# Cosformer attention into a gated feed-forward: the opening block's sums, copies and gate products in another order

## The chip, the cores and the metric

The kernel runs on one core of one Trainium2 chip. The metric is the time of one execution on the device in microseconds (us), lower is better. The engines named here are PE (TensorE: matrix products, transposes, each with a weight load PEld), DVE (VectorE), ACT (ScalarE), POOL (GpSimd) and SP (SyncE, which here only issues transfers).

## The reference

Eight batches of eight heads, 576 positions, head width 64. The attention has no softmax: with r = max(x, 0), a row of q or k becomes 128 features, r times a cosine and r times a sine of its position. Then a feed-forward layer with a norm in front works on the 4608 x 512 result.

```python
q_p, k_p = phi(q, cos_w, sin_w), phi(k, cos_w, sin_w)      # 128 features
kv  = einsum('bhsf,bhsd->bhfd', k_p, v)
z   = sum(k_p, axis=2)
num = einsum('bhsf,bhfd->bhsd', q_p, kv)
den = einsum('bhsf,bhf->bhs', q_p, z)[..., None] + 1e-06
x   = (num / den) as 4608 x 512
xn  = x / sqrt(mean(x*x) + 1e-6) * rms_g
out = (silu(xn @ w_gate) * (xn @ w_val)) @ w_out           # 512 -> 1536 -> 512
```

## The kernel before

The order of every engine's work is written out by hand (`manual_schedule`): each engine takes its instructions in the order in which the program names them, and waits only for what the data and the buffers ask. The work goes in blocks of 512 rows: one for each batch, and one with the eight tails of 64 rows. A block in its steady form is 12 gate products and 12 value products (`gval_mm`, 4 matmuls of 512 columns each, through the PSUM banks `psG[0/1]` and `psV[0/1]`), a silu on ACT and a product on DVE for each (`gval_h`), and then 48 matmuls against `w_out`. The attention of the next batch is put between these by hand (`at`, `run`).

Block 0 has no such cover. Its attention has to be done before its first products, and the program text of the opening does it in this order.

- `k_phi` makes the features of k in nine parts `c` (cosine half on DVE, sine half on ACT, the last two sine halves on DVE). `z0_pe(c)` adds each up over the rows with a matmul against ones into two banks, `psC[1]` and `psV[1]`. `g_spread`, after part 4, spreads the norm weight over the partitions (12 small matmuls into `psC[0]`).
- `q_phi` and `q_tr_pe` make and turn the first two of the four row groups j of q. `q_tr_evac` on DVE copies them out.
- `z0_copy` (ACT, twice, L389) takes the sums out as a row; `kv0_pe` makes k'v for the four head pairs hp (72 matmuls, L404) in the two banks of `psA`; `z0_turn` (8 small matmuls, L394) puts the sums beside it; `kvz_evac` (ACT, L277) copies both banks.
- For each j: `nd0_pe` (numerator and denominator into `psA`, L426 and L432), `nd_post` = `nd_rec` + `nd_div` on DVE (L455, L467; x into `xt`), `x_sq` (square sum on ACT, the power -0.5 on POOL, L483 and L488), `x_norm` on DVE (L495), `x_tr_pe` (turn, PE, L514), `x_tr_evac` (copy into `xnT`, L279 or L277).
- `filler` is a matmul on zeros whose result nobody reads.

The products of block 0 start before all its rows are ready. They go in units, `units[i]` = row groups j0 to j1 and columns of w_gate and w_val: units 0 to 3 are rows 0 and 1 against column groups 0-4 and 4-8, units 4 to 7 are rows 2 and 3 together against two column groups each. `unit_mm(i, wg)` is the gate product of a unit into `psG[i % 2]`, `unit_mm(i, wv)` the value product into `psV[i % 2]`, `unit_silu` and `unit_h` are its ACT and DVE steps (L622, L626), and all the matmuls are on L611.

The weights come from HBM in three parts for each matrix, column groups 0-4, 4-8 and 8-12, all issued by POOL (L174) in one order with the loads of q, k and v: wg 0-4, wv 0-4, wg 4-8, wv 4-8, k of batch 1, wg 8-12, wv 8-12, q and v of batch 1, then w_out in three parts.

After unit 3 the order before was: units 4, 5, 6, 7, each gate product, value product, silu, product, then `gval_step` for column groups 8 to 11.

Of the kernel before, what the change touches and what calls it, by code (L numbers as in the profile page):

```python
# [9 lines left out]
FP32 = mybir.dt.float32  # L10
BF16 = mybir.dt.bfloat16
# [6 lines left out]
def kernel(  # L18
# [11 lines left out]
    nc = tc.nc  # L30
    B, H, S, D = q.shape
    DM = H * D
    DFF = moe_w_gate.shape[1]
    P = 128
    TB = 512
    HP = H // 2
    NC = S // 64
# [3 lines left out]
    NDT = DM // P  # L41
    NNT = DFF // P
    E = D + 1
    F = 2 * D
    assert B == 8 and H == 8 and S == 576 and D == 64 and DFF == 1536

    V, A, G = nc.vector, nc.scalar, nc.gpsimd
# [2 lines left out]
    one = ctx.enter_context(tc.tile_pool(name="one", bufs=1))  # L50
    ring = ctx.enter_context(tc.tile_pool(name="ring", bufs=5))
    two = ctx.enter_context(tc.tile_pool(name="two", bufs=2))
    three = ctx.enter_context(tc.tile_pool(name="three", bufs=3))
    four = ctx.enter_context(tc.tile_pool(name="four", bufs=4))
    six = ctx.enter_context(tc.tile_pool(name="six", bufs=6))
    ps = ctx.enter_context(tc.tile_pool(name="ps", bufs=1, space=bass.MemoryType.PSUM))

    psA = ps.tile([P, 2, 512], FP32, name="psA")
# [132 lines left out]
    def g_parts():  # L191
        rest = g4
        for i in range(3):
            V.tensor_copy(out=g3[:, i, :], in_=rest[:, :])
            if i < 2:
                V.tensor_tensor(
                    out=gres[:, i, :], in0=rest[:, :], in1=g3[:, i, :], op=ALU.subtract
                )
                rest = gres[:, i, :]
# [19 lines left out]
    load_kv("k", 1, eng=G)  # L219
    load_w(wg, moe_w_gate, 8, NNT)  # L220

    def g_spread(bank):
        for t in range(NDT):
            for i in range(3):
                nc.tensor.matmul(
                    bank[:, t * P : (t + 1) * P], lhsT=sel[:, t, :], rhs=g3[:, i, :],
                    start=(i == 0), stop=(i == 2),
                )

    ang = math.pi / 2.0 / float(S)  # L230
    fidx = one.tile([P, NTAB], FP32, name="fidx")
# [43 lines left out]
    def copy(eng, o, i):  # L275
        if eng is A:
            A.copy(out=o, in_=i)  # L277
        else:
            eng.tensor_copy(out=o, in_=i)  # L279
# [10 lines left out]
    def k_phi(eng, b, c, part, hps=(0, HP)):  # L290
        o = slice(0, D) if part == 0 else slice(D, F)
        f = cos_of if part == 0 else sin_of
        if wide(b):
            rows = rows_of(c)
            src = raw_kv("k", b)[0:rows, :, c * D : (c + 1) * D]
            phi(eng, kp5[0:rows, c, :, o], src, f(14 + c)[0:rows, :])
            return
        src = raw_kv("k", b)[:, hps[0] : hps[1], c * D : (c + 1) * D]
        phi(eng, kp[:, c, hps[0] : hps[1], o], src, f(c))
# [39 lines left out]
    def q_tr_evac(eng, b, j, bank):  # L339
        dst = bank.bitcast(BF16).rearrange("p (h s) -> p h s", h=H)  # L340
        copy(eng, qpT[:, :, j * P : (j + 1) * P], dst)
# [12 lines left out]
    kvzs = {}  # L354
# [21 lines left out]

    zbank = [psC[1], psV[1]]
    zrow = one.tile([1, 2, HP * F], BF16, name="zrow")

    def z0_pe(c):  # L380
        for g in range(2):
# [3 lines left out]
                start=(c == 0), stop=(c == NC - 1),  # L385
            )

    def z0_copy(g):
        A.copy(out=zrow[:, g, :], in_=zbank[g][0:1, :])  # L389

    def z0_turn():
        for hp in range(HP):
            for g in range(2):
                nc.tensor.matmul(  # L394
                    heads[:, g, hp, D:E], lhsT=zrow[:, g, hp * F : (hp + 1) * F],
                    rhs=ones[0:1, 0:1], start=False, stop=(hp == HP - 1),
                    skip_group_check=True,
                )

    def kv0_pe(hp):  # L400
        for c in range(NC):
            for g in range(2):
                lo, hi = 64 * g, 64 * g + 64
                nc.tensor.matmul(  # L404
                    heads[:, g, hp, 0:D], lhsT=kp[lo:hi, c, hp, :],
                    rhs=vv0[lo:hi, hp, c * D : (c + 1) * D],
                    start=(hp == 0 and c == 0), stop=False, skip_group_check=True,
                )

    def kvz_evac(eng, b):  # L410
        kvzs[b] = six.tile([P, 2, HP * E], BF16, name="kvzs", tag="kvzs")
        copy(eng, kvzs[b][:, :, :], psA[:, :, 0 : HP * E])
# [39 lines left out]
    def nd_rec(b, j):  # L452
        rec = four.tile([P, 2, HP], FP32, name="rec", tag="rec")
        if b == 0 and j < 4:
            V.reciprocal(out=rec[:, :, :], in_=heads[:, :, :, D])  # L455
        else:
            V.tensor_scalar(
                out=rec[:, :, :], in0=heads[:, :, :, D], scalar1=1e-6, scalar2=None, op0=ALU.add
            )
            V.reciprocal(out=rec[:, :, :], in_=rec[:, :, :])  # L460
        rec_of[(b, j)] = rec

    def nd_div(b, j):
        xt = xts[count["x"] % NXT]
        count["x"] += 1
        rec = rec_of[(b, j)]
        V.tensor_tensor(  # L467
            out=xt[:, 0:DM].rearrange("p (hp g d) -> p g hp d", g=2, d=D),
            in0=heads[:, :, :, 0:D],
            in1=rec[:, :, :].unsqueeze(3).to_broadcast([P, 2, HP, D]),  # L470
            op=ALU.mult,
        )
        x_of[(b, j)] = xt

    def nd_post(b, j):
        nd_rec(b, j)
        nd_div(b, j)
# [13 lines left out]
    def x_norm(b, j, cols=(0, DM)):  # L491
        if cols[0] == 0:
            xn_of[(b, j)] = four.tile([P, DM], BF16, name="xn", tag="xn")
        c = slice(*cols)
        V.scalar_tensor_tensor(  # L495
            out=xn_of[(b, j)][:, c], in0=x_of[(b, j)][:, c], scalar=rs_of[(b, j)][:, :],
            in1=gb[:, c], op0=ALU.mult, op1=ALU.mult,
        )
# [11 lines left out]
    def x_tr_pe(b, j, bank, ts=(0, NDT)):  # L510
        xn = xn_of[(b, j)]
        dst = bank.bitcast(BF16).rearrange("p (t s) -> p t s", s=P)
        for t in range(*ts):
            nc.tensor.transpose(dst[:, t, :], xn[:, t * P : (t + 1) * P], ident[:, :])  # L514

    def x_tr_evac(eng, b, j, bank, ts=(0, NDT)):
        dst = bank.bitcast(BF16).rearrange("p (t s) -> p t s", s=P)
        copy(eng, x_dst(b, j)[:, ts[0] : ts[1], :], dst[:, ts[0] : ts[1], :])
# [20 lines left out]

    def gval_h(blk, n):  # L540
        g, v = banks_of(blk, n)
        sg = three.tile([P, TB], FP32, name="sg", tag="sg")
        A.activation(out=sg[:, :], in_=g[:, 0:TB], func=AF.Silu)  # L543
        V.tensor_tensor(out=hT[:, n, :], in0=v[:, 0:TB], in1=sg[:, :], op=ALU.mult)  # L544

# [21 lines left out]
    def filler(n, bank):  # L567
        for _ in range(n):
            nc.tensor.matmul(
                bank[:, :], lhsT=warm[:, 0:P], rhs=warm[:, :], start=True, stop=True  # L570
            )


    g_parts()
    filler(10, psC[1])
    for c in range(NC):
        k_phi(V, 0, c, 0)
        k_phi(A if c < 7 else V, 0, c, 1)
        z0_pe(c)
        if c == 4:  # L580
            g_spread(psC[0])
    qbank = [psG[0], psG[1], psV[0], psV[1]]
    for j in range(2):
        q_phi(V, 0, j, 0)
        q_phi(A, 0, j, 1)
        q_tr_pe(0, j, qbank[j])
    for j in range(2):
        q_tr_evac(V, 0, j, qbank[j])
    z0_copy(0)
    z0_copy(1)  # L590
    A.copy(out=gb[:, :], in_=psC[0][:, :])
    for hp in range(HP):
        kv0_pe(hp)
    z0_turn()
    kvz_evac(A, 0)

# [19 lines left out]
            )  # L618

    def unit_silu(i):  # L620
        sg_of[i] = three.tile([P, TB], FP32, name="sg", tag="sg")
        A.activation(out=sg_of[i][:, :], in_=psG[i % 2][:, 0:TB], func=AF.Silu)  # L622

    def unit_h(i):
        j0, j1, n0, n1 = units[i]
        V.tensor_tensor(  # L626
            out=hT[:, n0:n1, j0 * P : j1 * P],
            in0=psV[i % 2][:, 0:TB].rearrange("p (n s) -> p n s", n=n1 - n0),
            in1=sg_of[i][:, :].rearrange("p (n s) -> p n s", n=n1 - n0), op=ALU.mult,
        )  # L630

    HALF = DM // 2
    lo, hi = (0, NDT // 2), (NDT // 2, NDT)
    filler(3, psC[1])
    nd0_pe(0)
    q_phi(V, 0, 2, 0)
    q_phi(G, 0, 3, 0)
    q_phi(A, 0, 2, 1)
    q_phi(A, 0, 3, 1)
    filler(2, psC[1])  # L640
    nd_post(0, 0)
    q_tr_pe(0, 2, qbank[2])
    filler(1, psC[1])
# [1 line left out]
    load_w(wv, moe_w_val, 8, NNT)  # L645
    nd0_pe(1)
    q_tr_evac(V, 0, 2, qbank[2])
    filler(1, psC[1])
    q_tr_pe(0, 3, qbank[3])
    nd_post(0, 1)  # L650
    filler(2, psC[1])
    nd0_pe(2)
    x_sq(0, 1)
    load_q(1, eng=G)
# [4 lines left out]
    filler(1, psG[1])  # L659
    x_tr_pe(0, 0, psC[1], hi)  # L660
    x_tr_evac(A, 0, 0, psC[0], lo)
    q_tr_evac(A, 0, 3, qbank[3])
    nd_rec(0, 2)
    x_tr_evac(V, 0, 0, psC[1], hi)
    x_norm(0, 1)
    nd_div(0, 2)
    filler(2, psG[1])
    unit_mm(0, wg, by_rows=True)
    x_tr_pe(0, 1, psC[0])
# [5 lines left out]
    nd0_pe(3)  # L675
    nd_post(0, 3)
    x_norm(0, 2)
    unit_h(0)
    unit_mm(1, wg)
    unit_mm(1, wv)  # L680
    x_sq(0, 3)
# [1 line left out]
    load_wo(8, 12)  # L683
    unit_silu(1)
    x_norm(0, 3)
    x_tr_pe(0, 2, psC[1])
    x_tr_evac(V, 0, 2, psC[1])
    unit_h(1)
    unit_mm(2, wg)
    unit_mm(2, wv)  # L690
    x_tr_pe(0, 3, psC[0])
    x_tr_evac(V, 0, 3, psC[0])

    slots = {}

# [133 lines left out]
        out_store(A, blk, j, bank)  # L829
        run(blk, n, "post")  # L830

    for i in range(2, len(units)):
        if i > 2:
            unit_mm(i, wg)
            unit_mm(i, wv)
        unit_silu(i)
        unit_h(i)
        run(0, i, "post")
    for n in range(8, NNT):
# [37 lines left out]
```

## Time and profile before

| | us |
|---|---|
| median of 3 runs (lowest to highest) | 325.4 (324.87 to 326.1) |
| the profiled execution, its own time | 325.76 |
| its span, first to last instruction | 324.0 |
| PE busy in the span | 317.4 |
| DVE, ACT, POOL busy | 184.3, 165.2, 40.7 |

A timeline line gives start, duration, engine, source line, operation, output <- inputs and, in brackets, the idle time of the engine ahead of it and what ended it. Where one line stands for several instructions (x16), matmuls are pipelined: a group's duration is longer than the distance to the next group, and the distance is what the group costs PE.

### The profile page before, as it was taken

To read this page: it belongs to the slowest core of one execution; us is meant where nothing else is said; L and a number is where in the kernel's file an instruction comes from. 1 tells how busy PE (TensorE), PEld (TensorE's weight loads), DVE (VectorE), ACT (ScalarE), POOL (GpSimd) and SP (SyncE) were. 2 spreads that over 40 slices of the span, in tenths; PEclk is the share of its full clock that TensorE was granted. 3 is DMA by queue.
4 is the path that set the end of the run, shared out by engine and by line. 5 is a ranking of instruction groups with operands and counts; after the bars stand their busy time and mean duration, and the time that the engine had idled before them with its cause. 6 is when DMAs were issued, how large, how long until landed. Compare 5 with 4: busy or idle time off the path is not lost.

```text
span 324.0 us, 6128 instructions
## 1 busy us (share of the span) xinstructions
PE 317.4 (98%) x2348; PEld 163.7 (51%) x2348; DVE 184.3 (57%) x379; ACT 165.2 (51%) x319; POOL 40.7 (13%) x78
## 2 busy tenths in 40 slices
PE   7989999999999999999999999999999999999996
PEld 3679665544454445444454445444544444444444
DVE  7784858757727774576557745782577034204410
ACT  5664856754574547445754575446643343223321
POOL 9771212001000110011001000110011000000000
PEclk9999999999999999999999999999999999999999
DMA  7999995999579966998699958995822300041002
GB/s 228 231 266 273 281 327 212 228 204 259 125 178 216 231 193 159 200 229 210 171 205 214 211 149 182 223 200 144 134 49 41 123 32 0 2 98 32 2 32 97
DMA packets 77627, 53.37 MB, mean 165 GB/s; under 512 B 50410, under 2 KB 71326, under 8 KB 77598
## 3 DMA queue, kind: packets, MB, share of 16 engines
q1 hardware_dynamic: 70374, 39.81, 57.0%
q0 software_dynamic: 7216, 13.17, 16.5%
q8 instruction: 18, 0.29, 0.4%
q14 instruction: 11, 0.09, 0.1%
q10 hardware_dynamic: 8, 0.00, 0.0%
HBM read 37.83 MB, written 9.44 MB: 146 GB/s over the span
## 4 chain that ended last, share of the span: by engine, by line
PE 92%; DMA 5%; POOL 2%; issue 0%; DVE 0%; POOLq 0%
PE psC L547 27%; PE psG L524 27%; PE psV L524 27%; DMA wv<-in_moe_w_val_dram 5%; PE psA L417 2%; PE psG L547 2%; PE psA L361 2%; PE psV L611 2%; PE psG L611 1%; PE psA L368 1%; POOL raw L124 1%; PE psA L442 0%; POOL wg L174 0%; POOL vv L204 0%; PE psC L337 0%; PE psV L514 0%
## 5 line engine op out<-in xcount | busy, mean ns | idle before, releaser
L544 DVE TENSOR_TENSOR hT<-psV,sg 128x512 bf16<-128x512 f32 x100 | 68.9, 689 | 102.2 <-PE psV L524 65.9
L543 ACT ACTIVATE sg<-psG 128x512 f32<-128x512 f32 x100 | 59.2, 592 | 63.2 <-PE psG L524 63.2
L524 PE MATMUL psV<-xnT,wv 128*128 128x512 bf16 x352 | 90.3, 379 | 0.0
L524 PE MATMUL psG<-xnT,wg 128*128 128x512 bf16 x352 | 90.3, 379 | 0.0
L547 PE MATMUL psC<-wo,hT 128*128 128x512 bf16 (+1 forms) x408 | 89.1, 376 | 0.0
L547 PEld LDWEIGHTS <-hT 128*128 128x128 bf16 x456 | 42.8, 98 | 47.1
L524 PEld LDWEIGHTS <-wv 128*128 128x128 bf16 x400 | 39.1, 98 | 47.2
L524 PEld LDWEIGHTS <-wg 128*128 128x128 bf16 x400 | 37.1, 98 | 39.7
L488 POOL TENSOR_TENSOR rs<-ms,mhalf 128x1 f32<-128x1 f32 x36 | 19.8, 551 | 195.9 <-ACT scr L483 195.9
L277 ACT COPY osb<-psC 128x512 f32<-128x512 f32 x32 | 18.8, 586 | 50.0 <-PE psC L547 50.0
L483 ACT ACTIVATE scr<-xt 128x513 bf16<-128x513 f32 x36 | 22.8, 634 | 24.5 <-DVE xt L467 24.5
L495 DVE SCALAR_TENSOR_TENSOR xn<-xt,rs,gb 128x512 bf16<-128x512 f32 (+1 forms) x37 | 26.9, 730 | 9.7 <-POOL rs L488 9.7
L283 ACT ACTIVATE kp<-raw,tab 128x256 bf16<-128x256 f32 (+2 forms) x50 | 28.4, 609 | 2.5 <-DMA raw<-in_k_dram 2.5
L467 DVE TENSOR_TENSOR xt<-psA,rec 128x512 f32<-128x512 f32 x36 | 24.9, 691 | 1.2
L283 ACT ACTIVATE qp<-raw,tab 128x512 bf16<-128x512 f32 x32 | 22.6, 713 | 1.1 <-DMA raw<-in_q_dram 1.0
L285 DVE TENSOR_SCALAR kp<-raw,tab 128x256 bf16<-128x256 f32 (+2 forms) x54 | 20.3, 421 | 0.7 <-DMA raw<-in_k_dram 0.7
L285 DVE TENSOR_SCALAR qp<-raw,tab 128x512 bf16<-128x512 f32 x31 | 15.3, 498 | 1.6 <-DMA raw<-in_q_dram 1.6
L417 PEld LDWEIGHTS <-qpT 128*128 128x128 bf16 x224 | 10.5, 97 | 6.6 <-issue 0.5
L524 PE MATMUL psG<-xnT_tail,wg 128*128 128x512 bf16 x48 | 12.3, 379 | 0.0
L524 PE MATMUL psV<-xnT_tail,wv 128*128 128x512 bf16 x48 | 12.3, 379 | 0.0
L417 PE MATMUL psA<-kvzs,qpT 128*128 128x65 bf16 x224 | 11.4, 193 | 0.0
L279 DVE CAST vv<-raw 116x1280 bf16<-116x1280 f32 (+1 forms) x13 | 10.5, 805 | 0.0
(95 smaller groups left out, 181.0 us busy)
## 6 DMA issues: line engine op xcount, KB each, us to landing
out_dram<-osb SPq DMA_DIRECT2D x31, 256.0 KB, 2.4
raw<-in_k_dram SPq DMA_DIRECT2D x5, 1120.0 KB, 8.1
raw<-in_v_dram SPq DMA_DIRECT2D x5, 1120.0 KB, 7.7
raw<-in_q_dram SPq DMA_DIRECT2D x5, 1024.0 KB, 9.0
raw<-in_k_dram POOLq DMA_DIRECT2D x2, 1152.0 KB, 19.5
raw<-in_v_dram POOLq DMA_DIRECT2D x2, 1152.0 KB, 15.9
raw<-in_q_dram POOLq DMA_DIRECT2D x2, 1024.0 KB, 16.0
wg<-in_moe_w_gate_dram POOLq DMA_DIRECT2D x3, 512.0 KB, 14.7
```

What stands on the lines that cost most here:

```text
L277: A.copy(out=o, in_=i)
L283: A.activation(out=out_ap, in_=in_ap, func=AF.Relu, scale=scale)
L285: eng.tensor_scalar(out=out_ap, in0=in_ap, scalar1=scale, scalar2=0.0, op0=ALU.mult, op1=ALU.max)
L417: nc.tensor.matmul(heads[:, g, hp, :], lhsT=qpT[:, h, j * P : (j + 1) * P], rhs=kvzs[b][:, g, hp * E : (hp + 1) * E], start=True, stop=True,)
L467: V.tensor_tensor(out=xt[:, 0:DM].rearrange("p (hp g d) -> p g hp d", g=2, d=D), in0=heads[:, :, :, 0:D], in1=rec[:, :, :].unsqueeze(3).to ...
L483: A.activation(out=scr[:, :], in_=xt[:, 0 : DM + 1], func=AF.Square, scale=1.0 / math.sqrt(DM), accum_out=ms[:, :],)
L488: G.tensor_tensor(out=rs[:, :], in0=ms[:, :], in1=mhalf[:, :], op=ALU.pow)
L495: V.scalar_tensor_tensor(out=xn_of[(b, j)][:, c], in0=x_of[(b, j)][:, c], scalar=rs_of[(b, j)][:, :], in1=gb[:, c], op0=ALU.mult, op1=ALU. ...
L524: nc.tensor.matmul(bank[:, cols[0] : cols[1]], lhsT=w[:, t, n * P : (n + 1) * P], rhs=x[:, t, cols[0] : cols[1]], start=(t == 0), stop=(t ...
L543: A.activation(out=sg[:, :], in_=g[:, 0:TB], func=AF.Silu)
L544: V.tensor_tensor(out=hT[:, n, :], in0=v[:, 0:TB], in1=sg[:, :], op=ALU.mult)
L547: nc.tensor.matmul(bank[:, 0 : cols[1] - cols[0]], lhsT=hT[:, n, j * P : (j + 1) * P], rhs=wo[:, n, cols[0] : cols[1]], start=(n == 0), st ...
```

## The change

- `z0_copy` takes an engine: the sums in `psV[1]` are copied by DVE, those in `psC[1]` by ACT. `z0_turn` comes between the second and third head pair of `kv0_pe`.
- k'v and the sums of batch 0 are made in `psG[0]` and `psG[1]` and no longer in `psA`; each bank is copied by an engine of its own (`kvz0_evac`: ACT 0, DVE 1). The first two turns of q use the two banks of `psA` in their place.
- The sine half of k's part 7 moves from DVE to ACT.
- `g_spread` is cut into four parts of three matmuls, behind `z0_pe` of parts 0 to 3.
- The nine fillers between k'v and the turn of x's row group 0 are spread anew over their five places: 3, 2, 1, 1, 2 before; 2, 3, 1, 2, 1 after.
- `nd_rec(0, 2)` moves on DVE from ahead of the second half's `x_tr_evac` of row group 0 to behind `x_norm(0, 1)`.
- From unit 1 on: the gate products of units 2, 3 and 4 come ahead of the value products of units 2 and 3, the gate product of unit 5 ahead of the value product of unit 4. On DVE `unit_h(0)` goes behind the `x_tr_evac` of row group 2, `unit_h(1)` behind that of row group 3. The silu's ring has four buffers where it had three.

```diff
-    def g_spread(bank):
-        for t in range(NDT):
-            for i in range(3):
...
+    def g_spread(bank, t):
+        for i in range(3):
...
+    heads0 = [b[:, 0 : HP * E].rearrange("p (hp e) -> p hp e", e=E) for b in psG]
-    def z0_copy(g):
-        A.copy(out=zrow[:, g, :], in_=zbank[g][0:1, :])
+    def z0_copy(eng, g):
+        copy(eng, zrow[:, g, :], zbank[g][0:1, :])
...
+    def kvz0_evac(eng, g):
...
+        copy(eng, kvzs[0][:, g, :], psG[g][:, 0 : HP * E])
...
+    qbank = [psA[:, 0, :], psA[:, 1, :], psV[0], psV[1]]
-        k_phi(A if c < 7 else V, 0, c, 1)
+        k_phi(A if c < 8 else V, 0, c, 1)
         z0_pe(c)
-        if c == 4:
-            g_spread(psC[0])
-    qbank = [psG[0], psG[1], psV[0], psV[1]]
+        if c < NDT:
+            g_spread(psC[0], c)
...
-    for j in range(2):
-        q_tr_evac(V, 0, j, qbank[j])
-    z0_copy(0)
-    z0_copy(1)
+    z0_copy(V, 1)
+    z0_copy(A, 0)
+    q_tr_evac(V, 0, 0, qbank[0])
+    q_tr_evac(V, 0, 1, qbank[1])
     A.copy(out=gb[:, :], in_=psC[0][:, :])
-    for hp in range(HP):
-        kv0_pe(hp)
+    kv0_pe(0)
+    kv0_pe(1)
     z0_turn()
-    kvz_evac(A, 0)
+    kv0_pe(2)
+    kv0_pe(3)
+    kvz0_evac(A, 0)
+    kvz0_evac(V, 1)
...
+    x_tr_evac(V, 0, 0, psC[1], hi)
     q_tr_evac(A, 0, 3, qbank[3])
-    nd_rec(0, 2)
-    x_tr_evac(V, 0, 0, psC[1], hi)
     x_norm(0, 1)
-    nd_div(0, 2)
+    nd_post(0, 2)
...
     x_norm(0, 2)
-    unit_h(0)
     unit_mm(1, wg)
     unit_mm(1, wv)
...
     x_norm(0, 3)
+    unit_mm(2, wg)
     x_tr_pe(0, 2, psC[1])
     x_tr_evac(V, 0, 2, psC[1])
-    unit_h(1)
-    unit_mm(2, wg)
-    unit_mm(2, wv)
+    unit_silu(2)
+    unit_h(0)
+    unit_mm(3, wg)
     x_tr_pe(0, 3, psC[0])
     x_tr_evac(V, 0, 3, psC[0])
+    unit_silu(3)
+    unit_h(1)
+    unit_mm(4, wg)
+    for i in range(2, 4):
+        unit_mm(i, wv)
+        unit_h(i)
+    unit_silu(4)
+    unit_mm(5, wg)
+    unit_mm(4, wv)
+    unit_silu(5)
+    unit_h(4)
...
-    for i in range(2, len(units)):
-        if i > 2:
+    for i in range(5, len(units)):
+        if i > 5:
             unit_mm(i, wg)
-            unit_mm(i, wv)
-        unit_silu(i)
+            unit_silu(i)
+        unit_mm(i, wv)
         unit_h(i)
```

More of the change, by code (lines that the diff above doesn't have):

```diff
@@ L52 @@
     two = ctx.enter_context(tc.tile_pool(name="two", bufs=2))
-    three = ctx.enter_context(tc.tile_pool(name="three", bufs=3))
     four = ctx.enter_context(tc.tile_pool(name="four", bufs=4))
@@ L220 @@
     load_w(wg, moe_w_gate, 8, NNT)
-    def g_spread(bank):
-        for t in range(NDT):
-            for i in range(3):
[L225 to L228, printed above, removed]
+    def g_spread(bank, t):
+        for i in range(3):
+            nc.tensor.matmul(
+                bank[:, t * P : (t + 1) * P], lhsT=sel[:, t, :], rhs=g3[:, i, :],
+                start=(i == 0), stop=(i == 2),
+            )
     ang = math.pi / 2.0 / float(S)
@@ L394, in z0_turn @@
                 nc.tensor.matmul(
-                    heads[:, g, hp, D:E], lhsT=zrow[:, g, hp * F : (hp + 1) * F],
-                    rhs=ones[0:1, 0:1], start=False, stop=(hp == HP - 1),
-                    skip_group_check=True,
+                    heads0[g][:, hp, D:E], lhsT=zrow[:, g, hp * F : (hp + 1) * F],
+                    rhs=ones[0:1, 0:1], start=False, stop=False, skip_group_check=True,
                 )
@@ L404, in kv0_pe @@
                 nc.tensor.matmul(
-                    heads[:, g, hp, 0:D], lhsT=kp[lo:hi, c, hp, :],
+                    heads0[g][:, hp, 0:D], lhsT=kp[lo:hi, c, hp, :],
                     rhs=vv0[lo:hi, hp, c * D : (c + 1) * D],
-                    start=(hp == 0 and c == 0), stop=False, skip_group_check=True,
-                )
+                    start=(hp == 0 and c == 0), stop=(hp == HP - 1 and c == NC - 1),
+                    skip_group_check=True,
+                )
+    def kvz0_evac(eng, g):
+        if 0 not in kvzs:
+            kvzs[0] = six.tile([P, 2, HP * E], BF16, name="kvzs", tag="kvzs")
+        copy(eng, kvzs[0][:, g, :], psG[g][:, 0 : HP * E])
     def kvz_evac(eng, b):
@@ L541, in gval_h @@
         g, v = banks_of(blk, n)
-        sg = three.tile([P, TB], FP32, name="sg", tag="sg")
+        sg = four.tile([P, TB], FP32, name="sg", tag="sg")
         A.activation(out=sg[:, :], in_=g[:, 0:TB], func=AF.Silu)
@@ L620, in unit_silu @@
     def unit_silu(i):
-        sg_of[i] = three.tile([P, TB], FP32, name="sg", tag="sg")
+        sg_of[i] = four.tile([P, TB], FP32, name="sg", tag="sg")
         A.activation(out=sg_of[i][:, :], in_=psG[i % 2][:, 0:TB], func=AF.Silu)
@@ L633 @@
     lo, hi = (0, NDT // 2), (NDT // 2, NDT)
-    filler(3, psC[1])
+    filler(2, psC[1])
     nd0_pe(0)
@@ L639 @@
     q_phi(A, 0, 3, 1)
-    filler(2, psC[1])
+    filler(3, psC[1])
     nd_post(0, 0)
@@ L647 @@
     q_tr_evac(V, 0, 2, qbank[2])
-    filler(1, psC[1])
+    filler(2, psC[1])
     q_tr_pe(0, 3, qbank[3])
     nd_post(0, 1)
-    filler(2, psC[1])
+    filler(1, psC[1])
     nd0_pe(2)
```

## The prediction

> **What bounds the kernel now.** I read the page's chain first, then the chain piece by piece, then the timelines of PE, DVE and ACT from 8 to 35 us. The page gives the chain to PE, with one transfer in it.
>
> ```profile
> PE 92%; DMA 5%; POOL 2%; issue 0%; DVE 0%; POOLq 0%
> ```
>
> Piece by piece, the opening's place in the chain (start, length, what):
>
> ```profile
> 6.87 0.74 POOL wg L174
> 7.61 16.79 DMA wv<-in_moe_w_val_dram
> 24.40 0.05 issue
> 24.45 1.07 PE psV L611 x16
> ```
>
> So the second part of w_val, issued at 7.61, lands at 24.40, and from there to the end the chain is PE's own work. Nothing ahead of 24.40 that is not that transfer sets the time now. PE's timeline shows what it costs; the windows answer (PE, PEld, DVE, ACT, POOL busy, granted clock, DMA share) shows that PE is full afterwards.
>
> ```profile
> 20.29 1.05 PE L611 MATMUL psG<-xnT,wg 128*128 128x128 bf16 x16
> 21.18 1.06 PE L611 MATMUL psV<-xnT,wv 128*128 128x128 bf16 x16
> 22.12 0.40 PE L514 MATMUL psC<-ident,xn 128*128 128x128 bf16 x4
> 22.35 1.06 PE L611 MATMUL psG<-xnT,wg 128*128 128x128 bf16 x16
> 24.45 1.07 PE L611 MATMUL psV<-xnT,wv 128*128 128x128 bf16 x16 [1.04 <-DMA wv<-in_moe_w_val_dram]
> 25.35 0.39 PE L514 MATMUL psC<-ident,xn 128*128 128x128 bf16 x4
> 25.57 1.06 PE L611 MATMUL psG<-xnT,wg 128*128 128x128 bf16 x16
> ...
> 30.85 1.04 PE L611 MATMUL psG<-xnT,wg 128*128 128x256 bf16 x8
> ```
>
> ```profile
> 25.50:31.00 5.50, 5.50 (x71) 5.13 (x69) 2.41 (x4) 2.02 (x4) 0.76 (x1) 1.00 1.20 249
> ```
>
> A unit of 16 matmuls takes PE 0.89 us (20.29 to 21.18), one of 8 wide ones 0.87, four turns 0.22. Unit 2's gates start at 22.35 and are issued by 23.24; its values start at 24.45. The hole is 1.21 us, the only PE wait over 0.33 us behind 5.6 us. After it unit 6 starts at 30.85 and PE has no other wait on an engine or transfer.
>
> **Part 1, ahead of the units (to 17.87): worth nothing.** The second half of q arrives late, and DVE and ACT both stand still for it:
>
> ```profile
> 13.41 0.48 DVE L285 TENSOR_SCALAR qp<-raw,tab 128x512 bf16<-128x512 f32 x1 [1.64 <-DMA raw<-in_q_dram]
> 13.94 0.21 DVE L455 RECIPROCAL rec<-psA 128x8 f32<-128x8 f32 x1
> ```
>
> ```profile
> 12.76 0.59 ACT L277 CAST kvzs<-psA 128x520 bf16<-128x520 f32 x1 [0.97 <-PE psA L394]
> ```
>
> - The copy of k'v in two halves: DVE copies 128x256 f32 from PSUM in 0.42 and 128x128 in 0.29 (osb rows), so 260 columns take 0.43; ACT's 128x128 and 128x512 take 0.27 and 0.59, so 260 take 0.38. Both end by 13.19, where the one copy ended at 13.35: 0.16 earlier for `nd0_pe(0)`. But DVE's next step, `nd_rec(0, 0)`, stands behind the `q_phi` that waits for q until 13.41 and runs to 13.9. It starts at 13.94 all the same. Gain 0; 0.16 if q came earlier in another execution.
> - `z0_copy` on DVE: like DVE's 128x512 copy from PSUM, 0.69, from 9.95 (after `q_phi`) to 10.64. The two q copies behind it (0.65 apart) end at 11.95 where they ended at 11.76. Their reader, `nd0_pe(0)`, is at 13.2: cover 1.2. `z0_turn` comes after 36 of 72 k'v matmuls, at 10.97 + 0.7 = 11.7, 1.0 after its rows. Cost 0. Without the cover it would be 0.19.
> - k's part 7 on ACT (0.49, in ACT's idle 1.02 ahead of 9.03) takes 0.35 from DVE, but both then wait for q's first half at 9.03. `g_spread` in parts is the same 12 matmuls, 0.77 in all (7.59 to 8.36), and PE waits ahead of 9.80 for ACT's q features anyway. Gain and cost 0.
> - The fillers: nine in both. One less ahead of `nd0_pe(2)` saves up to 0.2 there, but the second half of `x_norm(0, 0)`, which DVE ends at 17.26, sets the turns at 17.33 and so unit 0. 0 again.
> - `nd_rec(0, 2)`, 0.21, ran in a DVE idle of 0.25 (waiting for turns at 17.64); now it is behind `x_norm(0, 1)` and pushes `nd_div(0, 2)` to 19.45 and the copy of row group 1 to 19.46 to 19.88. Readers: unit 1's gates at 20.29 (cover 0.36), `nd0_pe(3)` at 19.99 (cover 0.5), `x_sq(0, 2)`, 0.2 later, and behind it on POOL the first issue for w_out, 20.9. Its landing takes 20.0 to 21.1, so by 42.0; it is read from 43.95. The two later w_out issues follow `x_sq(0, 3)` and w_val's landing, which stay; the second can land at 43.96 (22.86 + 21.1), is read from 44.8 and after the gain below from 44.3. POOL's other queue and SP's are as before.
>
> **Part 2, the units.** From unit 1's value products at 21.18, with the distances above:
>
> - unit 2 gates 22.07 to 22.96. Part 4-8 of w_gate must be there: issued at 6.80, w_gate's median landing 14.7, so 21.5; in the trace it is only sure that it was there at 22.35 (0.28 is the bound on a loss here).
> - turns of row group 2 to 23.19, unit 3 gates to 24.08, turns of row group 3 to 24.30.
> - unit 4's gates need row group 3 copied. DVE's queue now:
>
> ```profile
> 22.93 0.75 DVE L495 SCALAR_TENSOR_TENSOR xn<-xt,rs,gb 128x512 bf16<-128x512 f32 x1 [0.27 <-POOL rs L488]
> 23.60 0.42 DVE L279 COPY xnT<-psC 128x512 bf16<-128x512 bf16 x1
> 23.93 0.68 DVE L626 TENSOR_TENSOR hT<-psV,sg 128x512 bf16<-128x512 f32 x1
> 25.77 0.42 DVE L279 COPY xnT<-psC 128x512 bf16<-128x512 bf16 x1 [1.16 <-PE psC L514]
> ```
>
> The first three keep their times (the product is now unit 0's). The last was 0.2 behind the end of its turns (25.57), so it is possible from 24.50, free at 24.54, done at 24.96. PE goes on 0.05 later (as 13.35 to 13.40): 25.01. **A new hole of 0.71** (24.30 to 25.01) takes the place of the old. Of it 0.67 is the copy's own latency; only 0.04 is the product ahead in DVE's queue. This copy was hidden behind unit 3 before; that cover is gone.
>
> - From 25.01: unit 4 gates 0.87, unit 2 values 0.89 (start 25.88, 1.48 after w_val's landing), unit 3 values 0.89, unit 5 gates 0.87, unit 4 values 0.87, unit 5 values 0.87: 5.26. Unit 6 starts at 30.27, not 30.85. No bank holds it: unit 2's values need `unit_h(0)` (24.6), unit 4's need `unit_h(2)` (27.7, used at 28.5).
>
> Sum: 0.58 earlier on PE, which then runs full, so the span goes from 324.0 to 323.4 and the profiled 325.76 to 325.2. That execution is 0.36 above the median. If its surplus was a late w_val, the median of before had a hole of 0.85, while the new hole does not depend on w_val until it is 1.5 later; then the new time is 325.2 as well. If the surplus was elsewhere, it is 324.8. I take 325.0.
>
> **A rule weighed.** The row: granted clock 1.00 in every window, the one with the 1.21 hole too; the first fillers follow each other at 0.43 until 4.04 and at about 0.22 afterwards, so PE's start is half as fast. The Trainium skill, "TensorE: Matmul & The Clock Gate", "A second HAM failure mode: psum-queue depth-cycling", speaks against the change: frequent small idle stretches between groups that cycle through PSUM banks can let the clock fall. The page's window is about 3.4 us, so one fall would cost about 1.7 by its figures, an estimate. I keep the row's answer: a longer hole left the clock up.
>
> **The rivals.**
> - *The wait comes back elsewhere* (0.17): w_gate's part lands nearer 22.35, or w_out's second part holds PE at 44.3, or the copy of row group 3 is late by 0.3 to 0.5. For it: DMA share 1.0 to 1.2 all through, the covers are 0.3 to 0.6. Then 325.3 to 325.8, 325.5.
> - *The hole closes altogether* (0.08): the copy hides and the whole 1.21 is gained: 324.2 against the median, 324.55 by the profiled run. Against: the copy's latency alone is 0.67.
> - *Slower: PE's clock falls in the opening* (0.15). Place: PE now ends the sums at about 9.1 and idles 0.7 to 9.8, where it idled 0.33; a second idle of 0.71 is at 24.3. Price from the first fillers: 1.17 to 4.04, 2.87 us, at half speed is 1.4 lost. One such stretch behind 17.87 makes 325.0 + 1.4 = 326.4, two 327.8. It decides once turns follow each other at twice the 0.056 of now (0.89 for 16). Against: the 0.7 idle from 4.85 to 5.55 and the hole of 1.21 brought none.
>
> **How the numbers follow.** The forecast, 324.6 to 325.4, has 0.60. The range goes from the closed hole at 324.2 to one slow stretch at 326.5; what is left out is part of the slow case and scatter. Half a per cent, 1.63 us, is about what a measurement of this kernel can tell from no change: faster means under 323.8, which even the closed hole misses, 0.07 for an earlier chain that I do not see; slower means over 327.0, most of the slow case, 0.12; within, 0.81.
>
> **What would show it.** Right: no PE wait on w_val; a PE gap of about 0.7 ahead of unit 4's gates, released by DVE's copy on L277 of the new file; unit 0 still at about 17.9; unit 6 near 30.3; no idle after. Wrong: unit 0 starts over 0.3 away from 17.87, unit 4's gates after 25.6, PE idle beyond 31, or distances of 0.43 between 512-column matmuls after 5 us.

## The result, and the profile after

The changed kernel takes 324.9 us (median of 22 runs, 324.42 to 325.51), the kernel before 325.42 (22 runs, 324.79 to 326.3): a ratio of 0.9982, 95% interval 0.9974 to 0.999. That is 0.52 us or 0.16% faster by the medians: within the half per cent that the prediction called no change, and yet the interval leaves 1 out. The profiled execution took 324.66 with a span of 322.9.

The page's chain, by engine, after. The w_val transfer was 5% of it. Now 2% is a transfer (q's), and 2% is DVE:

```profile
PE 93%; DMA 2%; DVE 2%; issue 1%; POOL 0%; ACT 0%; ACTq 0%; POOLq 0%
```

The chain piece by piece (start, length, what) names the new links. Where w_val's transfer stood, there is now the way of x's row group 3: its norm, its turn's copy, and between them in DVE's queue the product of unit 0.

```profile
21.81 0.57 POOL rs L492
22.41 0.75 DVE xn L499
23.16 0.33 DVE xnT L277
23.49 0.60 DVE hT L633
24.09 0.34 DVE xnT L277
24.48 1.05 PE psG L618 x8
```

PE's timeline from unit 1's value product on:

```profile
20.66 1.06 PE L618 MATMUL psV<-xnT,wv 128*128 128x128 bf16 x16
21.55 1.06 PE L618 MATMUL psG<-xnT,wg 128*128 128x128 bf16 x16
22.45 0.39 PE L518 MATMUL psC<-ident,xn 128*128 128x128 bf16 x4
22.67 1.06 PE L618 MATMUL psG<-xnT,wg 128*128 128x128 bf16 x16
23.56 0.39 PE L518 MATMUL psC<-ident,xn 128*128 128x128 bf16 x4
24.48 1.05 PE L618 MATMUL psG<-xnT,wg 128*128 128x256 bf16 x8 [0.53 <-DVE xnT L277]
25.36 1.95 PE L618 MATMUL psV<-xnT,wv 128*128 128x128 bf16 x32
27.15 1.04 PE L618 MATMUL psG<-xnT,wg 128*128 128x256 bf16 x8
28.02 1.91 PE L618 MATMUL psV<-xnT,wv 128*128 128x256 bf16 x16
29.77 1.04 PE L618 MATMUL psG<-xnT,wg 128*128 128x256 bf16 x8
```

The last line is unit 6. The turns of row group 3 are issued by 23.56 + 0.22 = 23.78, unit 4's gates start at 24.48: a hole of 0.70, released by DVE's copy. No wait on w_val is left; unit 2's values follow unit 4's gates without one (25.36). Behind it PE has no wait on another engine or a transfer, as before.

One thing in this profile misleads. Unit 0 starts at 17.46, 0.41 earlier than in the profile of before, and it is tempting to credit the opening's edits with it. Timelines of ACT, before and after (the first q features):

```profile
9.03 1.33 ACT L283 ACTIVATE qp<-raw,tab 128x512 bf16<-128x512 f32 x2 [1.02 <-DMA raw<-in_q_dram]
```

```profile
8.62 1.33 ACT L281 ACTIVATE qp<-raw,tab 128x512 bf16<-128x512 f32 x2 [0.38 <-DMA raw<-in_q_dram]
```

q's first half itself landed 0.41 earlier. Whether the change did that is the first question for the experiments.

### The profile page after: what moved, and what is told of

Its sections match the earlier page's. It is cut to its first block, busy times and chain, and to the rows that moved or that the text cites. A ratio compares the mean times of both kernels' runs of the same rounds, so it can differ in the third digit from the quotient of the medians.

```text
span 322.9 us, 6078 instructions
## 1 busy us (share of the span) xinstructions
PE 315.6 (98%) x2312; PEld 163.5 (51%) x2348; DVE 185.5 (57%) x380; ACT 164.9 (51%) x319; POOL 40.6 (13%) x78
## 4 chain that ended last, share of the span: by engine, by line
PE 93%; DMA 2%; DVE 2%; issue 1%; POOL 0%; ACT 0%; ACTq 0%; POOLq 0%
PE psV L528 27%; PE psC L551 27%; PE psG L528 26%; PE psA L421 2%; DMA raw<-in_q_dram 2%; PE psG L551 2%; PE psV L618 2%; PE psA L359 2%; PE psG L618 1%; PE psA L366 1%; DVE xn L499 1%; PE psV L335 0%; PE psA L446 0%; DVE xt L471 0%; PE psG L402 0%
## 5 line engine op out<-in xcount | busy, mean ns | idle before, releaser
L528 PE MATMUL psG<-xnT,wg 128*128 128x512 bf16 x338 | 88.6, 379 | 0.6 <-issue 0.2
```

Source lines behind the costliest of these rows:

```text
L528: nc.tensor.matmul(bank[:, cols[0] : cols[1]], lhsT=w[:, t, n * P : (n + 1) * P], rhs=x[:, t, cols[0] : cols[1]], start=(t == 0), stop=(t ...
```

## The experiments

Theory A: the order of the units makes the whole gain, by putting a hole of 0.70 where one of 1.2 to 1.3 was; the opening's edits are worth nothing; when q lands is scatter. Rival B: the opening's edits moved q's landing. Rival C: the removed hole is mostly smaller than the profile shows. Rivals D and E are in the expectations.

The profiles of all kernels, in us. "q" is the start of the first q features on ACT, units 0 and 6 are the starts of their gate products, the hole is PE's gap ahead of unit 2's values (in before's order, and with unit 2's values first) or ahead of unit 4's gates; it is counted from the time by which PE has issued what stands in front (the idle in a line's brackets starts up to 0.17 later, at the modelled end of the last matmul). The last two rows are the last experiment.

| kernel | q | unit 0 | unit 6 | q to unit 0 | unit 0 to 6 | hole | span less q |
|---|---|---|---|---|---|---|---|
| before | 9.03 | 17.87 | 30.85 | 8.84 | 12.98 | 1.21 | 315.0 |
| before, again | 8.37 | 17.32 | 30.30 | 8.95 | 12.98 | 1.31 | 315.0 |
| opening's edits alone | 9.16 | 17.97 | 30.98 | 8.81 | 13.01 | 1.34 | 314.9 |
| changed kernel | 8.62 | 17.46 | 29.77 | 8.84 | 12.31 | 0.70 | 314.3 |
| units' order alone | 8.90 | 17.75 | 30.06 | 8.85 | 12.31 | 0.70 | 314.3 |
| before, no wait on w_val | 8.76 | 17.61 | 29.27 | 8.85 | 11.66 | none | 313.6 |
| changed, no wait for row group 3 | 8.79 | 17.61 | 29.22 | 8.82 | 11.61 | none | 313.5 |
| unit 2's values first | 8.73 | 17.56 | 29.36 | 8.83 | 11.80 | 0.18 | 313.8 |
| changed kernel, again | 8.94 | 17.76 | 30.07 | 8.82 | 12.31 | 0.70 | 314.3 |
| unit 2's values first, again | 8.27 | 17.24 | 28.99 | 8.97 | 11.75 | 0.08 | 313.8 |
| before, no wait for q's second half | 8.78 | 17.62 | 30.33 | 8.84 | 12.71 | 0.90 | 314.7 |
| opening's edits, no wait for q's second half | 9.03 | 17.63 | 30.56 | 8.60 | 12.93 | 0.89 | 314.7 |

**The kernel before once more**, unchanged.

> The kernel before once more, for its profile alone. Theory A (the new order of the units made the gain; the 0.41 us by which unit 0 started earlier in the changed kernel's profile is scatter of q's transfers): the two halves of q may start the q features anywhere from 8.6 to 9.1 and 13.0 to 13.4 us, unit 0 follows at 17.4 to 17.9, and w_val's second part lands 23.5 to 24.5. Rival B (the opening's edits made q land earlier): q's features start at 9.03 and 13.41 again, within 0.05, and unit 0 at 17.87.

Measured: 325.21. q's features start at 8.37 and 12.86 and unit 0 at 17.32, with no edit at all. PE's line at w_val:

```profile
23.89 1.07 PE L611 MATMUL psV<-xnT,wv 128*128 128x128 bf16 x16 [1.15 <-DMA wv<-in_moe_w_val_dram]
```

q came 0.66 earlier than in the first profile, earlier than in the changed kernel's, and w_val came earlier with it (the products that waited for it start at 23.89, not 24.45). Rival B's ground is gone: the 0.41 is within what two profiles of one kernel differ by.

**The units' order alone.** The kernel before with the last part of the change's diff (from `x_norm(0, 2)` on) and the silu's ring of four:

```diff
+    unit_mm(2, wg)
     x_tr_pe(0, 2, psC[1])
     x_tr_evac(V, 0, 2, psC[1])
-    unit_h(1)
-    unit_mm(2, wg)
-    unit_mm(2, wv)
+    unit_silu(2)
+    unit_h(0)
+    unit_mm(3, wg)
     x_tr_pe(0, 3, psC[0])
...
```

> The kernel before with the new order of the units alone (gate products of 2, 3, 4 ahead of value products 2, 3; the silu's ring of four), its opening as it was. A: nearly the whole gain, 0.4 to 0.6 us under before, 324.8 to 325.0; no PE wait on w_val, a hole of about 0.7 ahead of unit 4's gates. B: only what is not the opening's 0.41, so 0.1 to 0.2 under before.

Measured: 324.93 against 325.34 of before on the same chip, ratio 0.9989 (0.998 to 0.9998). Its wait, from PE's waits (who, for what: us in total, times, longest), and its place:

```profile
PE psG L610 <- DVE xnT L278: 0.5, 1, 0.5
```

```profile
24.77 1.05 PE L610 MATMUL psG<-xnT,wg 128*128 128x256 bf16 x8 [0.54 <-DVE xnT L278]
```

The same 12.31 from unit 0 to unit 6, the same hole. This is the change's gain, all of it that a profile can resolve.

**The opening's edits alone.** The changed kernel with the order of the units of before (the same part of the diff, taken back; the silu's ring of four stays).

> The changed kernel with the order of the units of before: the opening's edits alone. A: within 0.15 us of before; PE waits for w_val as before, 0.7 to 1.2. B: 0.3 to 0.5 us faster, if w_val's landing moves with q's; if it does not, the same as before with a longer wait on w_val.

Measured: 325.33 against 325.34, ratio 1.0 (0.9991 to 1.0009). A holds; PE waits for w_val longer than ever:

```profile
24.57 1.07 PE L618 MATMUL psV<-xnT,wv 128*128 128x128 bf16 x16 [1.18 <-DMA wv<-in_moe_w_val_dram]
```

**The kernel before without the wait.**

```diff
     def unit_mm(i, w, by_rows=False):
+        sh = 4 if i == 2 and w is wv else 0
...
-                lhsT=w[:, t, n * P : (n + 1) * P],
+                lhsT=w[:, t, (n - sh) * P : (n - sh + 1) * P],
```

> The kernel before, in which unit 2's value product reads w_val's columns 0-4, which landed long before, in place of 4-8 (so a part of h is another product). It takes the wait on w_val away and nothing else. A: faster by the mean hole, 0.85 to 1.2 us, 324.2 to 324.6. Rival C (the hole is mostly smaller than in the one profile, since w_val lands earlier in other executions): 0.3 to 0.7 faster.

Measured: 324.3 against 325.34, ratio 0.9971 (0.996 to 0.9983). Unit 2's values follow its gates without a wait:

```profile
21.98 1.06 PE L612 MATMUL psG<-xnT,wg 128*128 128x128 bf16 x16
22.87 1.06 PE L612 MATMUL psV<-xnT,wv 128*128 128x128 bf16 x16
```

That is 1.04 faster by the medians (0.55 to 1.30 by the interval) and 1.32 by the distance from unit 0 to 6. Rival C, in which the hole is mostly smaller than in the one profile, falls in its strong form, a gain of 0.3 to 0.7: three profiles of the old order have holes of 1.21, 1.31 and 1.34, although q moved by 0.8 between them. Its direction is not excluded, since in the two profiles of the last experiment the hole is 0.90 and 0.89, and 1.04 lies between.

**The changed kernel without its new hole.**

```diff
     def unit_mm(i, w, by_rows=False):
+        sh = 2 if i == 4 and w is wg else 0
...
-                rhs=xnT[0][:, t, j0 * P : j1 * P],
+                rhs=xnT[0][:, t, (j0 - sh) * P : (j1 - sh) * P],
```

> The changed kernel, in which unit 4's gate product reads row groups 0 and 1 in place of 2 and 3 (so a part of h is another product): it does not wait for the copy of row group 3. A: the new hole of 0.7 us goes and nothing takes its place, since w_val lands 6.55 us after unit 0's start and unit 2's values then start 7.2 after it: unit 6 starts 11.65 us after unit 0, 324.2 to 324.4, 1.0 to 1.2 under before. Rival D (behind the hole another wait is next, w_val or a bank): 324.6 to 324.9.

Measured: 324.12 against 325.38 of before on the same chip, ratio 0.9963 (0.995 to 0.9977). Unit 4's gates follow the turns at once and unit 2's values follow them without a wait:

```profile
23.71 0.39 PE L518 MATMUL psC<-ident,xn 128*128 128x128 bf16 x4
23.94 1.04 PE L619 MATMUL psG<-xnT,wg 128*128 128x256 bf16 x8
24.81 1.95 PE L619 MATMUL psV<-xnT,wv 128*128 128x128 bf16 x32
```

12.31 becomes 11.61: the hole's 0.70, all of it, with no other wait behind it. Rival D falls for this place. So the change took 1.3 of waiting out and put 0.7 back in; nothing else moved by more than 0.1.

**Unit 2's values ahead of unit 4's gates.** The version that the two runs before point to: what PE has ready while DVE copies row group 3 is unit 2's value product, if its bank is free.

```diff
     x_norm(0, 2)
+    unit_h(0)
...
     unit_silu(2)
-    unit_h(0)
+    unit_h(1)
     unit_mm(3, wg)
...
     unit_silu(3)
-    unit_h(1)
-    unit_mm(4, wg)
-    for i in range(2, 4):
-        unit_mm(i, wv)
-        unit_h(i)
+    unit_mm(2, wv)
+    unit_h(2)
+    unit_mm(4, wg)
+    unit_mm(3, wv)
+    unit_h(3)
     unit_silu(4)
```

> A version of the change: unit 2's value product between the turn of row group 3 and unit 4's gate product, unit_h(0) and unit_h(1) back ahead of the copies of row groups 2 and 3 on DVE. A: the copy of row group 3 is hidden behind the value product, w_val's landing (6.55 us after unit 0's start) leaves a hole of 0.2 to 0.3 ahead of unit 2's values: unit 6 about 11.9 after unit 0, 324.3 to 324.5, faster than both kernels. Rival D: the wait on w_val is as long as the hole that it replaces (0.6 or more) and the time is the changed kernel's, 324.8 to 325.0.

Measured: 324.39 against 325.38, ratio 0.9973 (0.9963 to 0.9983): 0.99 under before where the change is 0.52 under it. PE's timeline:

```profile
23.67 0.39 PE L518 MATMUL psC<-ident,xn 128*128 128x128 bf16 x4
24.07 1.07 PE L618 MATMUL psV<-xnT,wv 128*128 128x128 bf16 x16
24.97 1.04 PE L618 MATMUL psG<-xnT,wg 128*128 128x256 bf16 x8
```

The turns are issued by 23.89, the values start at 24.07: a hole of 0.18, short of the 0.2 to 0.3 expected. PE's weight load (PEld) names what it waits for, w_val's second part:

```profile
24.07 0.90 PEld L618 LDWEIGHTS <-wv 128*128 128x128 bf16 x16 [0.19 <-DMA wv<-in_moe_w_val_dram]
```

The copy of row group 3 (24.11 to 24.52 on DVE) lies wholly beside it. The version's interval and the changed kernel's overlap, so both ran again, on one chip with the kernel before.

> The changed kernel once more, beside the version with unit 2's values first and the kernel before on one chip. A: 0.4 to 0.7 us under before; in the profile 12.31 from unit 0 to unit 6 and a span of 314.3 less q, wherever q lands.

> Unit 2's values ahead of unit 4's gates once more. A: 0.9 to 1.2 us under before and 0.4 to 0.6 under the changed kernel on the same chip; in the profile 11.8 to 11.9 from unit 0 to unit 6. Rival D: no measurable difference to the changed kernel (under 0.2).

Measured: before 325.51, the changed kernel 324.8 (ratio 0.9977, 0.9967 to 0.9987), the version 324.32 (0.9967, 0.9954 to 0.998): 0.71 and 1.19 under before, 0.48 apart. By the medians the version leads both times. The two intervals against before still overlap, and what sets the two kernels apart firmly is the profiles, 12.31 twice against 11.80 and 11.75 from unit 0 to unit 6.

**Is it q that hides the opening's edits?** Two kernels, one execution each: before, and the opening's edits alone, both with

```diff
-        phi(eng, qp_of((b, j))[:, :, o], raw_q(b)[:, :, j * D : (j + 1) * D], f(9 + j))
+        jj = j - 2 if b == 0 and j > 1 else j
+        phi(eng, qp_of((b, j))[:, :, o], raw_q(b)[:, :, jj * D : (jj + 1) * D], f(9 + j))
```

> The kernel before, in which the features of q's row groups 2 and 3 of batch 0 are made from groups 0 and 1 (so those rows are wrong): they do not wait for q's second half. Counted from the first q features on ACT: nd_rec(0, 0) at 4.85 (the one copy of k'v by ACT sets it, 4.9 before), unit 0 at 8.75 to 8.85.

> The opening's edits alone, with q's row groups 2 and 3 made from 0 and 1 in the same way. If q's second half hides the faster copy of k'v, as the prediction said: nd_rec(0, 0) 0.15 to 0.3 earlier than without the edits, 4.55 to 4.7 after the first q features, and unit 0 up to that much earlier, 8.55 to 8.7. Rival E (the copies in halves bring nothing even then): 4.85 and 8.8.

DVE's timelines around the copy of k'v, first without the edits, then with them:

```profile
11.44 0.69 DVE L285 TENSOR_SCALAR qp<-raw,tab 128x512 bf16<-128x512 f32 x1
13.69 0.21 DVE L456 RECIPROCAL rec<-psA 128x8 f32<-128x8 f32 x1 [1.56 <-PE psA L433]
```

```profile
12.67 0.43 DVE L277 CAST kvzs<-psG 128x260 bf16<-128x260 f32 x1 [0.30 <-PE psG L403]
13.01 0.68 DVE L283 TENSOR_SCALAR qp<-raw,tab 128x512 bf16<-128x512 f32 x1
13.61 0.19 DVE L460 RECIPROCAL rec<-psA 128x8 f32<-128x8 f32 x1
```

The first q features on ACT start at 8.78 and 9.03 in these two, so the reciprocal comes at 4.91 without the edits and at 4.58 with them, and unit 0 (17.62 and 17.63) at 8.84 and 8.60. So the edits do buy 0.24 up to unit 0 once q does not hide them, and rival E falls, by one profile each; in the ten other profiles this distance lies between 8.81 and 8.97. The gain is lost at once, at unit 0's value product, where PE's weight load waits for w_val's first part:

```profile
19.10 0.90 PEld L619 LDWEIGHTS <-wv 128*128 128x128 bf16 x16 [0.30 <-DMA wv<-in_moe_w_val_dram]
```

Unit 0's values start 10.09 after the first q features without the edits (18.87) and 10.07 with them, unit 1's gates 11.29 and 11.27. Behind that unit 2's values wait for w_val's second part in both, from 23.02 to 23.92 without the edits and from 23.26 to 24.15 with them:

```profile
24.15 1.07 PE L619 MATMUL psV<-xnT,wv 128*128 128x128 bf16 x16 [0.73 <-DMA wv<-in_moe_w_val_dram]
```

Their starts, 23.92 and 24.15, are 15.14 and 15.12 after the first q features, and the spans less q are 314.7 for both. In the old order of the units, then, the opening's edits stand behind three transfers in a row: q's second half and the first two parts of w_val.

## Why the prediction was right

- *What bounds the kernel.* Right: the wait on w_val was worth 1.32 from unit 0 to 6 when it was taken away. The prediction put it at 1.21, from a profile in which unit 0's value product started 0.1 late as well (19.09, behind turns issued by 18.99; that is 10.06 after the first q features, as in the last experiment, so w_val's first part is the likely cause). In the next two profiles of the old order the hole is 1.31 and 1.34, in the two of the last experiment 0.90 and 0.89.
- *Part 1, nothing.* Right, in sum (ratio 1.0) and in its reason: DVE's features of q's second half stand ahead of `nd_rec(0, 0)`. Counted from the first q features, that reciprocal came 0.13 sooner in the opening's edits alone (4.78 for 4.91), but DVE's next copy, of q's turned second half out of `psV`, came at 5.81 as before. Its estimates of the half copies, 0.43 on DVE and 0.38 on ACT, are the rows' 0.43 and 0.38, and `z0_copy` on DVE takes 0.67 for an estimated 0.69. One step in it failed without a price: the q copies were to end at 11.95. They start 1.27 after the first turn matmul (9.94), at the end of the last of the 16, where before they started 0.66 after it (10.46 from 9.80), with turns still running. `psA` is one tile with two banks where `psG` were two tiles, which would explain it; no run splits `psA`. DVE's line in the opening alone:

```profile
11.21 1.29 DVE L277 COPY qpT<-psA 128x1024 bf16<-128x1024 bf16 x2 [0.58 <-PE psA L335]
```

  They end at 12.50, 3.34 after the first q features where the estimate was 2.92. The cover was put at 1.2; the reader, `nd0_pe(0)`, is at 13.19, so 0.69 of it was left.
- *Part 2, the new hole of 0.71.* 0.70, with the same releaser and the copy where it was put (24.01, with the 0.41 of q's landing 24.42, for an estimated 24.54; 0.1 of the rest is unit 0's late values in the profile before).
- *The sum.* 0.58 predicted, 12.98 to 12.31 is 0.67; the missing 0.09 is that same 0.1 of the profile before, which made the removed hole look smaller. The medians of the three comparisons say 0.52, 0.71 and, for the units alone, 0.41; the first two intervals hold 0.67, the third ends at 0.65. The hole that was taken out may be smaller in some executions than in the first three profiles, as said.
- *From the profile to the median.* Two readings of the profiled run's 0.36 over the median were offered, a late w_val (then 325.2) or a surplus elsewhere (then 324.8). The repeated profile speaks for the second: q 0.66 earlier, w_val with it, the execution 0.55 shorter, and a hole of 1.31 all the same. For the median execution it stays open, since no trace shows its hole and two profiles have 0.9. The forecast of 325.0 lay between the two readings and 324.9 was measured; that it came out so close is in part luck.
- *The rule of the clock gate.* The Trainium skill, "TensorE: Matmul & The Clock Gate", "A second HAM failure mode: psum-queue depth-cycling", on clocks that fall after frequent small idle stretches: no run here shows it. Behind the hole of the changed kernel 8 wide matmuls take 0.88 (25.36 from 24.48) and 0.87 (28.02 from 27.15), ahead of it 16 narrow ones 0.89 (21.55 from 20.66), and PE's clock in the page stays at its top digit. The idle of 0.7 that the slower rival feared ahead of q's turns did come, 0.74 in the opening's edits alone (9.94, waiting for ACT's q features), with a hole of 1.34 behind it, and the clock stayed up there too. The rival had no event.
- *The signs.* One sign of being wrong did appear: unit 0 started at 17.46, 0.41 away from 17.87 where 0.3 was the limit, and unit 6 at 29.77, not near 30.3. The kernel before, run again, starts unit 0 at 17.32 with no edit, so the limit was narrower than the scatter of q's landing. Counted from unit 0, unit 6 came where the sum had it to 0.1 (12.31 for 12.40).
- *The chances and the half per cent.* The 0.12 for a time over 327.0 does not follow from the prediction's own price, by which one slow stretch ends at 326.4 and only two at 327.8. And a measurement here can tell less than half a per cent from no change: the interval of 0.9974 to 0.999 does.
- *The hole closes altogether.* It did not in the change. That work for closing most of it lay ready, unit 2's values, was not seen in the prediction.

## What to carry to other kernels

Taking a wait out of PE's queue by pulling work ahead is worth the old hole less the one that the pulled work itself meets: look up what its inputs wait for, down to the latency of the last copy. When the hole is a transfer's, look at which of the engine's later products are ready at each moment of it, not only which can be moved; here one further swap closed 0.5 of the 0.7 that was left. And where a profile differs from another by less than its transfers scatter, measure from a point behind the transfer: counted from the first q features, the spans of three profiles of the old order agree within 0.1 us (314.9 to 315.0), and so do three of the new order (314.3), while within each order the executions' times spread over up to 0.7 (325.21 to 325.88). It holds only as far as the later transfers keep their distance: in the two profiles of the last experiment w_val came 0.3 sooner after q, and they have 314.7.

## What the runs showed of the hardware that was not expected

The transfers' scatter is shared. In the twelve profiles the first q features start between 8.27 and 9.16 us, and w_val's second part, issued by POOL after q, v and three other parts of the weights, mostly comes with them: unit 2's values, where they wait for it in the order of before, start 15.42 (9.03 to 24.45), 15.52 (8.37 to 23.89), 15.41 (9.16 to 24.57), 15.14 and 15.12 after them, a spread of 0.4 where q's is 0.8. The 8.27 is not a landing: ACT is busy until 8.21 there and waits for nothing, so q may have come sooner. Why one execution's q is 0.9 us later than another's no run here tells.
